# A gated feed-forward block on one core: VectorE's first differences of x in halves, and in another order among its multiplications

## The chip, the core and the metric

The kernel runs on one core of a Trainium2 chip. The metric is the device time of one execution in microseconds (us), from launch to end. Engines are named as in the profile: PE is TensorE, which multiplies matrices; PEld is its loading of weights; DVE is VectorE; ACT is ScalarE; POOL is GpSimd; SP is SyncE, which here only issues DMAs. "L244" is line 244 of the kernel file.

## What is computed

The reference, cut to what matters, with x of 2048 x 1024 (tokens x model width), w_gate and w_up of 1024 x 3584, w_down of 3584 x 1024, all bf16:

```
return (gelu(x @ w_gate) * (x @ w_up)) @ w_down
```

So for each token there are 3584 features; each needs a gate value and an up value, a Gelu of the gate and one multiplication. The last matrix product brings the features back to width 1024.

## The kernel before

**Tiling.** The tokens are taken in two halves of 1024 (`h` = 0, 1), each half as two token blocks of 512 (`tb` = 0, 1). x is held transposed in two tiles, `xT[0]` and `xT[1]`, one per token block: 128 partitions x 8 slices (`kd`) x 512 tokens. Features are taken in blocks of 128, two blocks ("a pair") at a time, so there are 14 pairs per half; weights come in chunks of four blocks, that is two pairs. After the 14 pairs of a half, `down_group` multiplies by w_down for each token block.

**Fewer products.** With the 8 slices of the model width split in two, the two feature blocks and the two token blocks, each pair is a 2 x 2 by 2 x 2 block product, for gate (`j` = 0) and for up (`j` = 1). `pair_quads` computes it in seven products of blocks instead of eight (m1 to m7, four matmuls of 128x128 by 128x512 per product and `j`). The price is sums of blocks. On the side of x there are five, made once per half by `t_sum`, each 128 x 2048 elements in 32-bit form in `t_mem`. With b(j, l) the slices of width half j and token block l: T1 = b(0,1) - b(0,0); T2 = b(1,1) - T1; T3 = b(1,1) - b(0,1); T4 = b(1,0) - T2; and b22, a copy of b(1,1) in 32-bit form. VectorE makes T1 to T4 (L244), ScalarE the copy (L236). On the side of the weights there are S1 to S4 per pair and `j`, of 128 x 512 elements (`s_sum`), made by GpSimd (L365) as a rule, by VectorE (L363) for the first S3, and a copy a22 by ScalarE (L378). The products use them so: m5 is S1 with T1, m6 is S2 with T2, m7 is S3 with T3, m3 is S4 with b22, m4 is a22 with T4, and m1 and m2 use weights and x as they are.

**The first pair.** In half 0, pair 0 is computed without these sums by `first_pair_units` (L311 to L333), since the sums need the whole of x and x is still arriving. It has four units: two feature blocks (`u`) for token block 0, then the same two for token block 1. Each unit holds two of the eight PSUM banks, one for gate and one for up. `part` issues the matmuls (L249): 32 for token block 0, with banks 2, 3 and 6, 7, and 32 for token block 1, with banks 4, 5 for unit 0 and 0, 1 for unit 1. `unit_out` finishes a unit: ScalarE's Gelu of the gate bank (L268), then VectorE's multiplication of that by the up bank into the tile hT (L273). Between them stand the calls of `t_sum`, and behind them the first calls of `s_sum`.

**The pair behind it.** Pair 1 starts with m1, whose result goes to bank 2 (gate) and bank 3 (up) and is then copied by ScalarE (L447) to bank 4 and bank 5. Then m2 is added to banks 2 and 3, so it has to wait for these copies; the copies in turn overwrite banks 4 and 5, which unit 0 of token block 1 still holds until its Gelu (bank 4) and its multiplication (bank 5) have read them:

```
for j in range(2):
    mm(P_[j], j, block(key, j, 0, 0), b11, True)                       # m1
    act(nc.scalar.copy(out=banks[QB[j]][:], in_=banks[P_[j]][:]))      # L447
...
        m2()
```

Then follow m5 (banks 0 and 1, which unit 1 of token block 1 held; copied to a tile by ScalarE, L438), m6 (banks 4 and 5; copied to banks 6 and 7 by ScalarE, L443), then on VectorE the additions of the m5 tile to banks 4 and 5 (L416), then m7, m3 (into banks 4 and 5 behind these additions) and m4. m2's own multiplication into hT and then T4 stand on VectorE's queue ahead of the additions.

**What sets the order.** Each engine runs its instructions in the order in which the calls are made: the helpers `pe`, `dve`, `act`, `pool` and `sp` chain every instruction behind the one before it on the same engine (`on`, L111). An instruction that waits holds up everything behind it on its engine. Waits between engines follow from the tiles that are read and written.

**Loads of x.** The first four slices of xT[0] are transposed by PE and copied out by VectorE (L301) and ScalarE (L303, the last one). The others come by transposing DMAs on SP's queue (L172): four single slices of xT[0], then xT[1] in three: slices 0 and 1, slices 2 and 3, slices 4 to 7.

Of the kernel before, what the change touches and what calls it, by code (L numbers as in the profile page):

```python
# [34 lines left out]
def kernel(  # L35
# [14 lines left out]
    KD = D // P  # L50
    KH = KD // 2
# [71 lines left out]
    def act(inst):  # L123
        return on("act", inst)

    def dve(inst):
        return on("dve", inst)
# [98 lines left out]
    def t_sum(name, c0=0, c1=KH):  # L226
        def b(j, l):
            return xT[l][:, j * KH + c0 : j * KH + c1, :]

        t0 = ("t1", "t2", "t3", "b22", "t4").index(name) * KH * TB  # L230
        t = t_mem[:, t0 : t0 + KH * TB].rearrange("p (a b) -> p a b", b=TB)
        tsum[name] = t
        t = t[:, c0:c1, :]
        if name == "b22":
            for c in range(c1 - c0):
                act(nc.scalar.copy(out=t[:, c, :], in_=b(1, 1)[:, c, :]))  # L236
            return
        in0, in1 = {
            "t1": lambda: (b(0, 1), b(0, 0)),
            "t2": lambda: (b(1, 1), tsum["t1"].bitcast(F32)[:, c0:c1, :]),  # L240
            "t3": lambda: (b(1, 1), b(0, 1)),
            "t4": lambda: (b(1, 0), tsum["t2"].bitcast(F32)[:, c0:c1, :]),
        }[name]()
        dve(nc.vector.tensor_tensor(out=t, in0=in0, in1=in1, op=ALU.subtract))  # L244


    def mm_gu(ps, w_sb, fi, tb, kd):
        pe(
            nc.tensor.matmul(  # L249
                ps[:],  # L250
                lhsT=w_sb[:, kd, fi * P : (fi + 1) * P],
                rhs=xT[tb][:, kd, :],
                start=(kd == 0),
                stop=(kd == KD - 1),
            )
        )
# [3 lines left out]
    def gelu(ps, last=False):  # L260

        if last:
            g_sb = o_pool.tile([P, TB], F32, name="o_sb")[:]
        else:
            e0 = 4 * CH + (g_ctr[0] % 4) * 2 * TB
            g_ctr[0] += 1
            g_sb = w_mem[:, e0 : e0 + 2 * TB].bitcast(F32)
        act(nc.scalar.activation(out=g_sb, in_=ps[:], func=ACT.Gelu_apprx_tanh))  # L268
        return g_sb

    def mult(hT, g_sb, ps, fc, tb):
        dve(
            nc.vector.tensor_tensor(  # L273
                out=hT[:, fc, tb * TB : (tb + 1) * TB],
                in0=g_sb,
                in1=ps[:],
                op=ALU.mult,
            )
        )

    def unit_out(hT, bset, fi, tb):
        mult(hT, gelu(banks[bset[0]]), banks[bset[1]], fi, tb)

    def transpose_x0(q):

        parts = [(2 * q, 0, 4), (2 * q + 1, 0, 4)]
        if q == 0:
            parts = [(0, 0, 2), (0, 2, 4), (1, 0, 4)]
        for n, (kd, ts0, ts1) in enumerate(parts):
            tp = banks[(PB + QB)[(2 * q + n) % 4]][:].bitcast(BF16)  # L290
            for ts in range(ts0, ts1):
                pe(
                    nc.tensor.transpose(
                        tp[:, ts * P : (ts + 1) * P],
                        xs0[:, ts, kd * P : (kd + 1) * P],
                        ident[:],
                    )
                )
            cols = slice(ts0 * P, ts1 * P)
            if q == 0 or n == 0:  # L300
                dve(nc.vector.tensor_copy(out=xT[0][:, kd, cols], in_=tp[:, cols]))  # L301
            else:
                act(nc.scalar.copy(out=xT[0][:, kd, cols], in_=tp[:, cols]))  # L303

    def part(held, tb, k0, k1, us=(0, 1)):
        for kd in range(k0, k1):
            for j in range(2):
                for u in us:
                    mm_gu(banks[held[u][j]], chunks[first][j], u, tb, kd)

    def first_pair_units(hT):  # L311

        held = (VB, RB)
        transpose_x0(0)
        part(held, 0, 0, 1)
        transpose_x0(1)
        part(held, 0, 1, KD)
        for u in range(2):
            unit_out(hT, held[u], u, 0)
        held = (QB, PB)  # L320
        part(held, 1, 0, KH)
        t_sum("t1")
        t_sum("t2")
        t_sum("b22")
        t_sum("t3")
        for u in range(2):
            part(held, 1, KH, KD, (u,))
            unit_out(hT, held[u], u, 1)
        for j in range(2):
            s_sum(0, 1, j, "s3", True, False)  # L330
        for name in ("s1", "s2", "s4"):
            for j in range(2):
                s_sum(0, 1, j, name)  # L333
# [10 lines left out]
    def s_sum(h, pair, j, name, on_dve=False, staged=True):  # L344
        key = (h, "p", pair)

        def a(i, kh):
            return block(key, j, i, kh)

        if on_dve and staged and name in ("s1", "s2", "s3"):  # L350

            if j == 0:
                first_s[name] = wd_pool.tile([P, WDT, D], BF16, name="wd_sb")
            t = first_s[name][:, j, :].bitcast(F32R)
        else:
            s0 = (2 * S_NAMES.index(name) + j) * KH * P
            t = s_mem[:, s0 : s0 + KH * P]
        t = t.rearrange("p (a b) -> p a b", b=P)
        ssum[(h, pair, j, name)] = t

        def tt(in0, in1, op):
            if on_dve:
                dve(nc.vector.tensor_tensor(out=t, in0=in0, in1=in1, op=op))  # L363
            else:
                pool(nc.gpsimd.tensor_tensor(out=t, in0=in0, in1=in1, op=op))  # L365

        if name == "s1":
            tt(a(1, 0), a(1, 1), ALU.add)
        elif name == "s2":
            s1 = ssum[(h, pair, j, "s1")].bitcast(F32)  # L370
            tt(s1, a(0, 0), ALU.subtract)
        elif name == "s3":
            tt(a(0, 0), a(1, 0), ALU.subtract)
        elif name == "s4":
            s2 = ssum[(h, pair, j, "s2")].bitcast(F32)
            tt(a(0, 1), s2, ALU.subtract)
        else:
            act(nc.scalar.copy(out=t, in_=a(1, 1)))  # L378
# [437 lines left out]
    for h in range(NH):  # L816
        hT = hT_pool.tile([P, KF, SH], BF16, name="hT")
        first_pair = 0
        if h == 0:
            first_pair_units(hT)  # L820
            first_pair = 1
            xs = [(tb, kd) for tb in (1, 0) for kd in range(KD)]
            new_x(1)
            stage_load(0)
            stage_load(1)
# [153 lines left out]
```

## Time and profile before

| what | value |
|---|---|
| median of 4 runs | 544.24 us (541.9 to 545.96) |
| the profiled execution: its own time | 545.96 us |
| the profiled execution: span, first to last instruction | 544.2 us |
| granted clock of TensorE | 1.000 |
| PE busy | 532.8 us, 98% of the span |
| DVE, ACT, POOL busy | 362.7, 263.1, 246.6 us |
| T sums on VectorE (L244), 128x2048 each | 2.28 to 3.24 us |
| multiplications of the first units (L273), 128x512 each | 0.67 to 0.69 us |

The profiled execution took 545.96 us, 1.76 us more than its span and 1.72 us more than the median. Of 544.2 us, PE is busy 532.8, so all idle time of PE is some 11 us, and the start and the end of the program hold a good part of that. The stretch that the change touches lies between 12 and 37 us of the span.

### The profile page before, as it was taken

The numbers are of one execution on the slowest core, as the hardware profiler recorded it, in microseconds if no ns is written. First come the engines' busy times: TensorE is split into PE (matmuls) and PEld (weight loads), VectorE is DVE, ScalarE is ACT, GpSimd is POOL, SyncE is SP. The second block draws the span as 40 slices with busy tenths as digits, with TensorE's granted clock in tenths as the row PEclk, the third lists the DMA queues.
The fourth block names the chain that finished last, engine by engine and source line by source line (L and its number), as shares of the span: only waits on it lengthen the run. The fifth ranks groups of instructions, "written<-read, shape, count | busy, mean of one in ns | idle before, by whom it ended". The sixth has DMA issues, their size and how long they took to land.

```text
span 544.2 us, 7084 instructions
## 1 busy us (share of the span) xinstructions
PE 532.8 (98%) x2348; PEld 377.0 (69%) x2384; DVE 362.7 (67%) x472; ACT 263.1 (48%) x446; POOL 246.6 (45%) x212
## 2 busy tenths in 40 slices
PE   8899999998999999999999999999999999999997
PEld 3477777776666677767677666777777766866865
DVE  0986777777676899689584343344444469969951
ACT  1555555554555317216565555555555552452270
POOL 0698777777677000000046777666677740000000
PEclk9999999999999999999999999999999999999999
DMA  9918686696736976879970405041322457677945
GB/s 217 320 33 261 151 275 208 200 275 179 254 125 214 296 236 217 312 226 298 327 233 1 155 1 156 0 155 28 127 87 69 148 187 227 229 243 244 287 148 203
DMA packets 84804, 102.70 MB, mean 189 GB/s; under 512 B 18720, under 2 KB 66336, under 8 KB 84768
## 3 DMA queue, kind: packets, MB, share of 16 engines
q1 hardware_dynamic: 61968, 80.30, 46.7%
q10 hardware_dynamic: 22800, 21.96, 13.1%
q8 instruction: 19, 0.31, 0.2%
q14 instruction: 17, 0.14, 0.1%
HBM read 85.98 MB, written 12.58 MB: 181 GB/s over the span
## 4 chain that ended last, share of the span: by engine, by line
PE 89%; DMA 4%; DVE 4%; issue 2%; ACT 0%; ACTq 0%; SPq 0%; DVEq 0%
PE bank L393 56%; PE bank L667 32%; DMA o_sb<-in_x_dram 2%; DVE t_mem L244 1%; DMA w_mem<-in_w_gate_dram 1%; DVE o_sb L602 1%; DMA w_mem<-in_w_up_dram 1%; DVE s_mem L363 1%; PE bank L249 0%; DVE hT L273 0%; DMA t_dram<-o_sb 0%; DMA x_dram<-o_sb 0%; DVE s_mem L642 0%; DVE bank L416 0%; ACT o_sb L720 0%
## 5 line engine op out<-in xcount | busy, mean ns | idle before, releaser
L393 PE MATMUL bank<-t_mem,s_mem 128*128 128x512 f32 x1056 | 250.0, 394 | 1.8 <-DVE bank L416 1.8
L393 PEld LDWEIGHTS bank<-t_mem,s_mem 128*128 128x128 f32 x1056 | 198.0, 188 | 46.3 <-issue 2.5
L365 POOL TENSOR_TENSOR s_mem<-w_mem 128x512 fp32r<-128x512 bf16 x102 | 121.1, 1209 | 193.8 <-DMA w_mem<-in_w_up_dram 103.3
L273 DVE TENSOR_TENSOR hT<-w_mem,bank 128x512 bf16<-128x512 f32 x104 | 71.0, 686 | 88.5 <-PE bank L393 47.0
L667 PE MATMUL bank<-t_mem,s_mem 128*128 128x512 f32 x544 | 127.2, 392 | 0.0
L667 PEld LDWEIGHTS bank<-t_mem,s_mem 128*128 128x128 f32 x544 | 102.1, 188 | 22.2 <-issue 0.2
L416 DVE TENSOR_TENSOR bank<-bank,m 128x512 f32<-128x512 f32 x108 | 69.6, 694 | 45.4 <-ACT m L438 44.3
L393 PE MATMUL bank<-xT,w_mem 128*128 128x512 bf16 x405 | 96.5, 380 | 3.2 <-ACT bank L447 1.8
L268 ACT ACTIVATE w_mem<-bank 128x512 f32<-128x512 f32 x104 | 61.7, 596 | 57.1 <-DVE bank L416 37.8
L393 PEld LDWEIGHTS <-w_mem 128*128 128x128 bf16 x432 | 40.2, 98 | 53.4 <-issue 8.7
L365 POOL TENSOR_TENSOR s_mem<-w_mem,s_mem 128x512 fp32r<-128x512 bf16 x52 | 65.8, 1290 | 0.0
L577 DVE TENSOR_TENSOR t_mem<-w_mem 128x1024 fp32r<-128x1024 bf16 x56 | 65.6, 1218 | 0.0
L365 POOL TENSOR_TENSOR s_mem<-s_mem,w_mem 128x512 fp32r<-128x512 f32 x52 | 62.3, 1219 | 0.0
L443 ACT COPY bank<-bank 128x512 f32<-128x512 f32 x54 | 30.8, 570 | 38.8 <-PE bank L393 38.5
L378 ACT CAST s_mem<-w_mem 128x512 fp32r<-128x512 bf16 x54 | 33.1, 616 | 31.0 <-PE bank L393 28.8
L642 DVE TENSOR_TENSOR s_mem<-hT 128x512 fp32r<-128x512 bf16 x52 | 35.1, 705 | 10.3 <-PE bank L667 9.5
L438 ACT COPY m<-bank 128x512 f32<-128x512 f32 x54 | 31.7, 587 | 18.0 <-PE bank L393 18.0
L667 PEld LDWEIGHTS <-hT 128*128 128x128 bf16 x224 | 21.3, 98 | 26.6 <-issue 2.1
L447 ACT COPY bank<-bank 128x512 f32<-128x512 f32 x54 | 30.8, 570 | 14.3 <-PE bank L393 12.2
L720 ACT CAST o_sb<-bank 128x512 bf16<-128x512 f32 x28 | 15.4, 585 | 39.9 <-PE bank L667 39.9
L602 DVE TENSOR_TENSOR o_sb<-wd_sb,o_sb 128x512 fp32r<-128x512 bf16 x28 | 29.1, 1038 | 0.5
L574 ACT CAST t_mem<-w_mem 128x1024 fp32r<-128x1024 bf16 x28 | 26.9, 1047 | 0.0
(42 smaller groups left out, 236.9 us busy)
## 6 DMA issues: line engine op xcount, KB each, us to landing
t_mem<-t_dram SPq DMA_DIRECT2D x56, 512.0 KB, 5.4
w_mem<-in_w_gate_dram ACTq DMA_DIRECT2D x10, 1024.0 KB, 5.5
w_mem<-in_w_up_dram ACTq DMA_DIRECT2D x10, 1024.0 KB, 8.6
wd_sb<-in_w_down_dram SPq DMA_DIRECT2D x28, 256.0 KB, 4.8
t_dram<-o_sb SPq DMA_DIRECT2D x28, 256.0 KB, 2.7
wd_sb<-in_w_down_dram SPq DMA_DIRECT2D x12, 512.0 KB, 8.1
w_mem<-in_w_down_dram SPq DMA_DIRECT2D x10, 512.0 KB, 6.2
w_mem<-in_w_down_dram SPq DMA_DIRECT2D x4, 1024.0 KB, 6.6
```

The source lines that it names most:

```text
L268: act(nc.scalar.activation(out=g_sb, in_=ps[:], func=ACT.Gelu_apprx_tanh))
L273: nc.vector.tensor_tensor(out=hT[:, fc, tb * TB : (tb + 1) * TB], in0=g_sb, in1=ps[:], op=ALU.mult,)
L365: pool(nc.gpsimd.tensor_tensor(out=t, in0=in0, in1=in1, op=op))
L378: act(nc.scalar.copy(out=t, in_=a(1, 1)))
L393: nc.tensor.matmul(banks[bank][:], lhsT=lhs[:, c, :], rhs=rhs[:, c, :], start=start and c == 0, stop=c == KH - 1, skip_group_check=True,)
L416: nc.vector.tensor_tensor(out=banks[dst][:], in0=banks[src][:], in1=m5[j][:], op=ALU.add)
L438: act(nc.scalar.copy(out=m5[j][:], in_=banks[V_[j]][:]))
L443: act(nc.scalar.copy(out=banks[RB[j]][:], in_=banks[QB[j]][:]))
L577: dve(nc.vector.tensor_tensor(out=t, in0=in0, in1=in1, op=ALU.subtract))
L602: dve(nc.vector.tensor_tensor(out=t, in0=in0, in1=in1, op=ALU.subtract))
L642: dve(nc.vector.tensor_tensor(out=t, in0=in0, in1=in1, op=op))
L667: nc.tensor.matmul(banks[bset[u]][:], lhsT=lhs(i, u), rhs=rhs(i), start=start and i == 0, stop=stop and i == NS - 1, skip_group_check=True,)
```

## The change

VectorE's queue in `first_pair_units` gets another order, and two of its sums are cut in halves by slices. T1 is made as two instructions of 128x1024 elements (slices 0 and 1, then 2 and 3) and placed ahead of the two multiplications of token block 0's units instead of behind them. T2 stays whole. T3 is also made in two halves: the first is ahead of unit 0's multiplication of token block 1, as the whole was, and the second is between unit 0's and unit 1's. VectorE's queue before: multiplication, multiplication, T1, T2, T3, multiplication, multiplication. After: T1 first half, T1 second half, multiplication, multiplication, T2, T3 first half, multiplication, T3 second half, multiplication. The queues of PE, ACT, POOL and SP hold the same instructions in the same order.

```diff
@@ -315,17 +315,20 @@
         part(held, 0, 0, 1)
         transpose_x0(1)
         part(held, 0, 1, KD)
+        t_sum("t1", 0, KH // 2)
+        t_sum("t1", KH // 2, KH)
         for u in range(2):
             unit_out(hT, held[u], u, 0)
         held = (QB, PB)
         part(held, 1, 0, KH)
-        t_sum("t1")
         t_sum("t2")
         t_sum("b22")
-        t_sum("t3")
-        for u in range(2):
-            part(held, 1, KH, KD, (u,))
-            unit_out(hT, held[u], u, 1)
+        t_sum("t3", 0, KH // 2)
+        part(held, 1, KH, KD, (0,))
+        unit_out(hT, held[0], 0, 1)
+        t_sum("t3", KH // 2, KH)
+        part(held, 1, KH, KD, (1,))
+        unit_out(hT, held[1], 1, 1)
         for j in range(2):
             s_sum(0, 1, j, "s3", True, False)
         for name in ("s1", "s2", "s4"):
```

## The prediction, as it was put on record

> **What bounds the kernel now.** I read the page's busy shares first: PE is busy 532.8 of 544.2 us, at a granted clock of 1.000 throughout, so only PE's gaps can be won. PE's list of waits has six entries, of which two lie where the change is: 1.8 us "<-ACT bank L447" and 0.3 us "<-DVE bank L416" (the latter line also has one of 1.4 us, at 132.9 us). Then PE in order of time (start, duration, what, idle before it and what ended it):
>
> ```profile
> 21.07 2.55 PE L393 MATMUL bank<-xT,w_mem 128*128 128x512 bf16 x11
> 25.46 1.02 PE L393 MATMUL bank<-xT,w_mem 128*128 128x512 bf16 x4 [1.85 <-ACT bank L447]
> 26.14 5.89 PE L393 MATMUL bank<-t_mem,s_mem 128*128 128x512 f32 x24
> 32.36 3.89 PE L393 MATMUL bank<-t_mem,s_mem 128*128 128x512 f32 x16 [0.34 <-DVE bank L416]
> ```
>
> These are m1 and half of m2, the other half of m2, m5 to m7, and m3 with m4 of pair 1. VectorE, and then ScalarE's two L447 rows, over the same stretch:
>
> ```profile
> 14.35 1.29 DVE L273 TENSOR_TENSOR hT<-w_mem,bank 128x512 bf16<-128x512 f32 x2 [7.15 <-PE bank L249]
> 15.55 2.28 DVE L244 TENSOR_TENSOR t_mem<-xT,xT 128x2048 fp32r<-128x2048 bf16 x1
> 17.87 3.13 DVE L244 TENSOR_TENSOR t_mem<-xT,t_mem 128x2048 fp32r<-128x2048 bf16 x1
> 20.92 3.24 DVE L244 TENSOR_TENSOR t_mem<-xT 128x2048 fp32r<-128x2048 bf16 x1
> 24.08 1.27 DVE L273 TENSOR_TENSOR hT<-w_mem,bank 128x512 bf16<-128x512 f32 x2
> 25.27 3.15 DVE L363 TENSOR_TENSOR s_mem<-w_mem 128x512 fp32r<-128x512 bf16 x2
> 28.34 0.68 DVE L273 TENSOR_TENSOR hT<-w_mem,bank 128x512 bf16<-128x512 f32 x1
> 28.94 2.67 DVE L244 TENSOR_TENSOR t_mem<-xT,t_mem 128x2048 fp32r<-128x2048 bf16 x1
> 31.53 2.48 DVE L416 TENSOR_TENSOR bank<-bank,m 128x512 f32<-128x512 f32 x4
> ```
>
> ```profile
> 22.19 0.57 ACT L447 COPY bank<-bank 128x512 f32<-128x512 f32 x1 [0.54 <-PE bank L393]
> 24.84 0.57 ACT L447 COPY bank<-bank 128x512 f32<-128x512 f32 x1 [2.08 <-DVE hT L273]
> ```
>
> VectorE is idle for 7.15 us up to 14.35, then has no gap until 35.4. The multiplication of unit 0, token block 1, starts at 24.08 although its Gelu was done at 19.93, because T2 and T3 stand ahead of it. ScalarE's second copy waits 2.08 us for it, and PE waits for that copy. The chain of waits runs through VectorE's rows from 14.95 to 32.23 and returns to PE at 32.36. So VectorE's queue is the bound from 14 to 32 us, and PE is the bound behind it.
>
> **Why T2, T3 and T4 take 2.7 to 3.2 us where T1 takes 2.28.** GpSimd's rows:
>
> ```profile
> 17.53 1.32 POOL L365 TENSOR_TENSOR s_mem<-w_mem 128x512 fp32r<-128x512 bf16 x1 [16.22 <-DMA w_mem<-in_w_gate_dram]
> 19.31 2.69 POOL L365 TENSOR_TENSOR s_mem<-w_mem 128x512 fp32r<-128x512 bf16 x1 [0.47 <-DMA w_mem<-in_w_up_dram]
> 21.97 4.31 POOL L365 TENSOR_TENSOR s_mem<-s_mem,w_mem 128x512 fp32r<-128x512 f32 x2
> ```
>
> Lay the ends side by side: GpSimd's first sum ends at 18.85, T2 at 21.00, GpSimd's second at 22.00, T3 at 24.16, GpSimd's third at 25.17. The differences are 2.15, 1.00, 2.16, 1.01: the two take strict turns, each blocked while the other works. T4 and both S3 fit the same pattern (S3's own part is 0.55). Multiplications, which read PSUM, keep their 0.6 us step beside GpSimd and take no turn. A sum by turns, then: 2.15 per whole T, 1.1 per half, 0.55 per S3, 1.03 per GpSimd sum.
>
> [...]
>
> **The change, part by part.** *T1 in halves, ahead.* Landing times: slices 0 and 1 of xT[1] were issued at 7.45 and took 4.8 (12.25), slices 2 and 3 at 8.89 and 4.2 (13.09), slices 4 to 7 at 10.24 and 4.7 (14.94). An uncontended 128x1024 sum of bf16 to 32 bits (L577) takes 1.22; half of T1's 2.28, 1.14, is the lower bound. So T1 runs 12.25 to 13.47 and 13.47 to 14.70, in the old idle time. The added waits are for these two landings (and for ScalarE's copy of slice 3 of xT[0], done at 8.73); queued behind them are the multiplications of token block 0, which slip from 14.35 to 14.65 and end at 15.9. Who waits for them: banks 3 and 7, wanted again by m1 at about 21.9 and by ScalarE's L443 copies at 29. That slip costs nothing, with 6 us of cover. T2 starts at 15.85 instead of 17.87, behind its landing of 14.94 and ahead of GpSimd's first sum (17.53), and ends at 18.13 uncontended. The cost of cutting T1 is 2 x 1.22 - 2.28 = 0.16 us of VectorE, in idle time.
>
> *T3 in halves.* GpSimd's first sum has its turn 18.13 to 19.15; T3's first half 19.15 to 20.25; GpSimd's second sum (weights landed at 19.3) 20.25 to 21.3. Unit 0's multiplication runs at 20.2, ends at 20.85, instead of 24.75. T3's second half waits for the turn until 21.3 and ends at 22.4; unit 1's multiplication (Gelu done at 21.65) ends at 23.0 instead of 25.35. The cost of this cut lies between 0 (halves of 1.08) and 0.16 plus one turn of 1.03; I take 0.05 plus the 0.5 that the turns give.
>
> *Behind it.* GpSimd's third sum 22.4 to 23.4, S3 to 23.95, GpSimd's fourth to 25.0, S3 to 25.55, GpSimd's fifth to 26.6, m2's multiplication beside it 25.5 to 26.15, T4 26.6 to 28.75, the addition into bank 4 to 29.35 (31.53 plus 0.62 was 32.15 before).
>
> *What PE sees.* ScalarE's second copy now waits only for m1 itself: in pair 2 the two copies start 0.80 apart (37.23, 38.03), so 22.19 + 0.80 + 0.57 = 23.56, and PE goes on at 23.61 instead of 25.46: **1.85 us** won. m5 follows at 24.3, its second half at 25.2 (bank 1 free at 23.0); m6 at 26.05 and 27.0 (GpSimd's S2 at 23.4 and 25.0); m7 at 27.9 (S3 at 25.55, T3 at 22.4). The last matmul of m7 started at 31.64; at their 0.22 step m3 could have started at 31.86 and did at 32.36. Now it could at 30.01, and the addition is done 0.66 earlier, so the second gap goes as well: **0.5 us** (0.34 listed, the rest hidden in the matmul's modelled end). m3's second half wants GpSimd's sixth sum, which slips from 29.46 to 29.8, at 30.9: covered by 1.1. Sum: 2.35.
>
> *Whether it lasts.* From 32.36 the chain is PE but for one stretch, 110 to 132.9 us. Pair 2's needs move with it: S1 of pair 2 is ready at 30.9 and 32.05, wanted at 35.3; its weights landed at 23.8 and 26.75, wanted at 33.75. The stretch from 110 to 132.9 (a transposing DMA of 9.01 us, a wait of 1.41 at PE) begins with a release by PE's matmuls at 109.9, so it shifts with them.
>
> **The sum.** On the profiled execution's own time: 545.96 - 2.35 = 543.6. It was the slowest of four runs, 1.72 above their median; the gaps won are early and set by fixed work, so I take the same gain off the median: 544.24 - 2.35 = **541.9 us**, or 0.43% less.
>
> **The rivals.**
> *A, half of it (542.6).* VectorE's queue slips where I gave it 0.66 us ahead of need, by a turn lost to GpSimd before T4 (1.03): the addition is then done at 30.4, m3 starts at 30.5. With two turns lost it is 31.5 and the gain 0.9. For it: T3's halves offer one more meeting. Against: every meeting in the trace alternates. Gain 0.9 to 1.9, middle 1.6.
> *B, hidden anyway (544.2).* Something not tied to PE sets a later point, so the gain is given back: the 9.01 us transposes at 116 us are the candidate. For: DMA stands in the chain there. Against: their issue stands behind PE's and VectorE's work in that chain.
> [...]
> *D, more.* The 1.41 us wait at 132.9 goes by luck of the DMAs: 540.5.
> That the queue does not take the written order is excluded: the order of VectorE's instructions in the changed kernel is as the change says, and the other queues are unchanged.
>
> **How the numbers follow.** Chances: forecast 0.60, A 0.18, B 0.12, C 0.05, D 0.05. The range reaches from just below D (540.3) to B (544.2), which takes in A with both its ends and leaves C out. A measurement of this kernel can tell about 0.5% (2.7 us) from no change; the forecast lies at 2.35, just inside, and the four runs spread over 4.06 us, so a median may stand about 1 us off. Faster by over 0.5% (below 541.5): 0.28 from the forecast, 0.03 from A, 0.05 from D, 0.36 in all. Slower by over 0.5% (above 547.0): 0.03, C with that scatter. Within: 0.61.
>
> **What would show it.** Right: L244's first row at 12.2 to 12.5, 128x1024; PE's wait of 1.85 on L447 gone and no L447 wait on L273; the wait at 32.36 gone, m3 at 30.0; the pairs behind it 2.3 us earlier up to 110. Wrong: T1's first half starting after 14 (a landing later than computed), T3's halves with more than one GpSimd sum between them, an addition (L416) that ends after 29.9, or a pair 2 that waits for S sums.

## The result and the profile after

The changed kernel takes 541.94 us (median of 40 runs), the kernel before 544.06 (66 runs). The ratio of the two is 0.997, with a 95% interval of 0.9958 to 0.9983. Of 544.06 us that is 1.6 us, between 0.9 and 2.3. The difference of the medians is 2.1. The runs of each kernel fall in two groups (before: 21 of 66 up to 542.75 us, the others from 543.18 on; changed: 21 of 40 up to 541.96, the others from 542.49 on), so the median of before lies in its upper group and that of the changed kernel in its lower one; the medians of the lower groups are 542.44 and 541.13, 1.3 us apart. On record stood 541.9 and a gain of 2.35.

The profiled execution of the changed kernel has a span of 541.8 us against 544.2. PE, pair 1 and the start of pair 2 (start, duration, what; a bracket would hold idle time before the row):

```profile
19.77 3.63 PE L396 MATMUL bank<-xT,w_mem 128*128 128x512 bf16 x15
23.05 9.52 PE L396 MATMUL bank<-t_mem,s_mem 128*128 128x512 f32 x40
32.41 1.90 PE L396 MATMUL bank<-xT,w_mem 128*128 128x512 bf16 x7
```

m1 and m2 are one row, m5 to m4 another, and neither row has idle time ahead of it. Both gaps of before (1.85 us at 25.46 and 0.34 at 32.36) are gone. VectorE over the same stretch, and below it ScalarE's two copies from m1's banks:

```profile
11.67 2.45 DVE L244 TENSOR_TENSOR t_mem<-xT,xT 128x1024 fp32r<-128x1024 bf16 x2 [4.45 <-DMA xT<-in_x_dram]
14.04 1.28 DVE L273 TENSOR_TENSOR hT<-w_mem,bank 128x512 bf16<-128x512 f32 x2
15.23 2.28 DVE L244 TENSOR_TENSOR t_mem<-xT,t_mem 128x2048 fp32r<-128x2048 bf16 x1
17.43 1.22 DVE L244 TENSOR_TENSOR t_mem<-xT 128x1024 fp32r<-128x1024 bf16 x1
18.66 0.69 DVE L273 TENSOR_TENSOR hT<-w_mem,bank 128x512 bf16<-128x512 f32 x1
19.26 1.49 DVE L244 TENSOR_TENSOR t_mem<-xT 128x1024 fp32r<-128x1024 bf16 x1
20.67 0.68 DVE L273 TENSOR_TENSOR hT<-w_mem,bank 128x512 bf16<-128x512 f32 x1
...
26.98 2.67 DVE L419 TENSOR_TENSOR bank<-bank,m 128x512 f32<-128x512 f32 x4
```

```profile
20.89 0.57 ACT L450 COPY bank<-bank 128x512 f32<-128x512 f32 x1 [0.54 <-PE bank L396]
21.70 0.57 ACT L450 COPY bank<-bank 128x512 f32<-128x512 f32 x1 [0.24 <-PE bank L396]
```

T1's halves lie in what was VectorE's idle time in the profile of before, up to 14.35. (Where token block 0 ends earlier, as in before_again below, VectorE is idle only up to 13.01, and they lie there in part.) Unit 0's multiplication is done at 19.35, so the second copy waits for PE alone, 0.81 behind the first. The additions begin 4.55 us earlier (26.98 against 31.53); 1.30 of that is an earlier start, which is told of next.

One thing in this profile is not the change's. Token block 0's first Gelu starts at 12.41, in the profile of before at 13.71. There PE had a wait of 0.9 us for up weights of the first chunk:

```profile
PE bank L249 <- DMA w_mem<-in_w_up_dram: 0.9, 1, 0.9
```

That transfer took 4.3 us from issue to landing; here it took 3.4, and PE's list has no such wait. So 36.10 - 32.41 = 3.69 us at pair 2 is made of 1.30 us of start and 2.39 us of change. From 132.88 against 129.54 on it is 3.34 (the transpose in the middle took 9.34 us instead of 9.01), and from 492 on 2.3 (a wait of PE of 0.8 us for a load of sums, which the profile of before has not).

To take the start out, I use one measure for all kernels below: **the stretch from token block 0's first Gelu (ScalarE, L268) to the first matmul of pair 2**. It is 22.39 us in the profile of before and 20.00 in that of the changed kernel, where PE has no gap in it.

### The profile page after: what moved, and what is told of

Same layout as the page of the kernel before. It is cut to its first block, busy times and chain, and to the rows that moved or that the text cites. A ratio compares the mean times of both kernels' runs of the same rounds, so it can differ in the third digit from the quotient of the medians.

```text
span 541.8 us, 7086 instructions
## 1 busy us (share of the span) xinstructions
PE 532.6 (98%) x2348; PEld 377.2 (70%) x2384; DVE 361.8 (67%) x474; ACT 263.3 (49%) x446; POOL 245.5 (45%) x212
## 4 chain that ended last, share of the span: by engine, by line
PE 91%; DMA 5%; DVE 2%; issue 1%; ACT 0%; SPq 0%; DVEq 0%; ACTq 0%
PE bank L396 58%; PE bank L670 31%; PE bank L249 2%; DMA o_sb<-in_x_dram 2%; DMA t_mem<-t_dram 1%; DVE o_sb L605 1%; DMA w_mem<-in_x_dram 1%; DMA t_dram<-o_sb 0%; DMA x_dram<-o_sb 0%; DVE hT L273 0%; DVE s_mem L645 0%; DVE s_mem L366 0%; ACT w_mem L268 0%; PE bank L293 0%; DVE t_mem L244 0%
## 5 line engine op out<-in xcount | busy, mean ns | idle before, releaser
L268 ACT ACTIVATE w_mem<-bank 128x512 f32<-128x512 f32 x104 | 61.8, 596 | 54.7 <-DVE bank L419 36.4
L368 POOL TENSOR_TENSOR s_mem<-s_mem,w_mem 128x512 fp32r<-128x512 f32 x52 | 61.2, 1197 | 0.0
L605 DVE TENSOR_TENSOR o_sb<-wd_sb,o_sb 128x512 fp32r<-128x512 bf16 x28 | 30.4, 1084 | 0.5
```

## The experiments

Two theories stood against each other. *Turns:* VectorE's queue ends late because its sums and GpSimd's take turns, and GpSimd's first sums start when their weights land (17.53 and 19.31 us in the profile of before), not when PE is ready; so the gain depends on when the start lets token block 0 end. *Constant gain:* the two gaps are worth 2.35 us always, and what is missing of it was lost later. Beside these stood the question which half of the change does it.

### T1 alone (t1_only)

```diff
-        t_sum("t3", 0, KH // 2)
-        part(held, 1, KH, KD, (0,))
-        unit_out(hT, held[0], 0, 1)
-        t_sum("t3", KH // 2, KH)
-        part(held, 1, KH, KD, (1,))
-        unit_out(hT, held[1], 1, 1)
+        t_sum("t3")
+        for u in range(2):
+            part(held, 1, KH, KD, (u,))
+            unit_out(hT, held[u], u, 1)
```

(against the changed kernel)

> Only T1 in halves ahead of token block 0's multiplications; T3 whole, where it was before. Theory (turns): VectorE's queue is what ends late, and T1 in the idle time takes 2.3 us out of it; where T3 is cut does not matter, since unit 0's multiplication is early enough either way (done at about 20.3 against 21.7 when ScalarE could copy). So the same as the whole change: 1.4 to 2.35 us faster than before, no wait of PE on the L447-copies or on the additions. Rival (each half of the change gives its share): about half the gain, 0.7 to 1.2 us, with a rest of PE's wait on the copy.

541.57 us against 542.68 for the kernel before on the same chip; ratio 0.9984 (0.9961 to 1.0007). PE has no wait in the stretch. In its profile the granted clock was 0.949 and the stretch 20.43 us long; pair 1's first 15 matmuls took 3.76 us there and 3.63 in the changed kernel, the 40 behind them 9.52 in both. I do not lay its length beside the others; the missing waits tell enough. The time alone can tell this neither from the whole change nor from no change.

### T3 alone (t3_only)

The changed kernel with T1 whole and back behind token block 0's multiplications.

> Only T3 in halves around unit 0's multiplication; T1 whole and behind token block 0's multiplications, as before. Theory (turns): unit 0's multiplication comes about 1 to 1.5 us earlier, so PE's first wait (on the L447-copy) goes wholly or mostly; but VectorE's queue ends where it did or a little later (one more instruction, one more turn), so the second wait, on the L416-additions, grows by as much: 0 us, between 0.3 faster and 0.3 slower. Rival (the copy's wait is the loss): 0.9 to 1.85 us faster.

543.51 against 542.68; ratio 1.0008 (0.9991 to 1.0025): no gain. PE:

```profile
20.32 3.63 PE L395 MATMUL bank<-xT,w_mem 128*128 128x512 bf16 x15
23.60 5.87 PE L395 MATMUL bank<-t_mem,s_mem 128*128 128x512 f32 x24
30.69 3.88 PE L395 MATMUL bank<-t_mem,s_mem 128*128 128x512 f32 x16 [1.22 <-DVE bank L418]
```

The wait on the copy is gone, and a wait of 1.22 us on the additions stands in its place. The stretch is 21.44 us. The first wait was what the profile named longest, but it was not what the queue cost: VectorE still did the same work from the same start, and PE met it 24 matmuls later, behind m5, m6 and m7.

### A late start made to order (before_late, after_late, t1_only_late)

```diff
         transpose_x0(1)
+        for _ in range(6):
+            pe(
+                nc.tensor.matmul(
+                    banks[0][:], lhsT=warm_l, rhs=warm_r, start=True, stop=True
+                )
+            )
         part(held, 0, 1, KD)
```

> The kernel before with six idle matmuls of 128x512 (1.3 us) on PE ahead of the last 28 matmuls of token block 0, results unused: token block 0 always ends about 1.3 us later than where the weights come early, and GpSimd's first sums stay where the weights' landing puts them. Theory (the gain depends on the start): 2.0 to 2.4 us slower than before in executions that had no wait for weights, so 1.3 to 2.3 over all; PE's waits on copy and addition as in the profile of before (1.85 and 0.34). Rival (constant gain): 1.3 us slower or less, and no more than its twin with the change loses.

> The changed kernel with the same six idle matmuls. Theory (the gain depends on the start): 1.3 us slower than the changed kernel at most, so 0.2 to 1 us faster than before, and 2.35 us faster than its twin without the change; no wait of PE on copy or addition. Rival (constant gain): the twin differs by what the kernels without idle matmuls differ by, 1.5 us.

> T1 alone in halves ahead, T3 whole, with the six idle matmuls on PE that put token block 0's end 1.3 us later. Theory (turns): T3's halves give nothing at a late start either; unit 0's multiplication is done at about 21.9 to 22.3 against 23.0 to 23.4 when ScalarE can copy, so the stretch from the first Gelu to pair 2 is 20.0 us, as with the whole change and the idle matmuls (19.99), and not 22.5 as without the change. Rival (T3's halves matter where the start is late): 20.4 to 21.5, with a rest of PE's wait on the L447-copy or the L416-additions.

| kernel | time | before, same chip | ratio (95%) | stretch |
|---|---|---|---|---|
| before_late | 545.76 | 542.68 | 1.005 (1.0029 to 1.007) | 22.53 |
| after_late | 542.10 | 542.68 | 1.0002 (0.9979 to 1.0026) | 19.99 |
| t1_only_late | 542.05 | 542.20 | 1.0000 (0.9984 to 1.0017) | 20.00 |

PE of before_late, with both gaps of the first profile again, then PE of t1_only_late:

```profile
25.82 1.02 PE L399 MATMUL bank<-xT,w_mem 128*128 128x512 bf16 x4 [1.77 <-ACT bank L453]
26.50 5.85 PE L399 MATMUL bank<-t_mem,s_mem 128*128 128x512 f32 x24
32.72 3.46 PE L399 MATMUL bank<-t_mem,s_mem 128*128 128x512 f32 x14 [0.37 <-DVE bank L422]
```

```profile
21.01 3.62 PE L400 MATMUL bank<-xT,w_mem 128*128 128x512 bf16 x16
24.29 9.53 PE L400 MATMUL bank<-t_mem,s_mem 128*128 128x512 f32 x40
```

In before_late, T2 (VectorE) and GpSimd's first sum:

```profile
18.09 3.27 DVE L244 TENSOR_TENSOR t_mem<-xT,t_mem 128x2048 fp32r<-128x2048 bf16 x1
18.05 1.15 POOL L371 TENSOR_TENSOR s_mem<-w_mem 128x512 fp32r<-128x512 bf16 x1 [16.75 <-DMA w_mem<-in_w_gate_dram]
```

GpSimd was ahead by 0.04 us, so T2 waited for its sum. By the ratios, 1.3 us of idle matmuls cost the kernel before 2.7 us (1.6 to 3.8; 1.3 to 2.3 were expected), while the changed kernel goes from 0.997 to 1.0002, some 1.7 us, on another chip and with an interval of 1.3 us to either side. The stretches of before_late and its twin after_late differ by 2.54 us and their ratios by 0.0048, which is 2.6 (their medians by 3.66, more than the stretch explains). Each of these ratios is uncertain by 1.1 to 1.3 us, so the times alone leave room for the 1.5 of the rival; the stretches decide. At a late start T1 alone does all that the whole change does, and this with a profile at a granted clock of 1.000: T3's halves add nothing that shows.

### The kernel before, twice more (before_again, before_again2)

> The kernel before, unchanged, for another profile of it. Measured from the first Gelu of token block 0 (ScalarE, L268) to the first matmul of pair 2, the profile of before takes 22.39 us and that of the changed kernel 20.00, in which PE has no gap. Theory (the gain depends on the start): where token block 0 ends early (first Gelu at 12.4), this stretch is 21.4, since GpSimd's turns stay where the weights' landing puts them, so 1.4 is left to win; where it ends at 13.7 or later, 22.3 to 22.5. Rival (constant gain): 22.4 either way.

> The same kernel once more, for a third profile of it, with the same two expectations: 21.4 us with an early end of token block 0 and 22.4 with a late one, against 22.4 either way.

One execution of each, of 546.28 and 542.35 us. First Gelus at 12.38 and 12.73, pair 2 at 33.92 and 34.28: stretches of 21.54 and 21.55, as the first theory has it, so what sets the two executions 3.9 us apart lies outside the stretch. PE in the first of them, and below it T2 and T3 with GpSimd's first two sums:

```profile
19.74 2.55 PE L393 MATMUL bank<-xT,w_mem 128*128 128x512 bf16 x11
23.29 1.02 PE L393 MATMUL bank<-xT,w_mem 128*128 128x512 bf16 x4 [1.01 <-ACT bank L447]
23.97 5.88 PE L393 MATMUL bank<-t_mem,s_mem 128*128 128x512 f32 x24
30.18 3.89 PE L393 MATMUL bank<-t_mem,s_mem 128*128 128x512 f32 x16 [0.33 <-DVE bank L416]
```

```profile
16.54 2.29 DVE L244 TENSOR_TENSOR t_mem<-xT,t_mem 128x2048 fp32r<-128x2048 bf16 x1
18.75 3.24 DVE L244 TENSOR_TENSOR t_mem<-xT 128x2048 fp32r<-128x2048 bf16 x1
18.00 5.00 POOL L365 TENSOR_TENSOR s_mem<-w_mem 128x512 fp32r<-128x512 bf16 x2 [16.69 <-DMA w_mem<-in_w_gate_dram]
```

The first gap is 1.01 us, not 1.85: VectorE's queue started 1.34 us earlier, T2 was under way when GpSimd's first weights landed, and of T2 and T3 only T3 had to wait for a turn. T2 takes 2.29 us instead of 3.13, and these 0.84 us are the difference of the stretches (21.54 against 22.39); in before_late they are 3.27 and 22.53. So of 2.39 us to win, 1.54 are left. Of the eleven profiles of kernels without idle matmuls, the one that the prediction rests on is the only one in which PE itself sits idle for these weights (in before_again, before_again2, the changed kernel and after_again its loading of weights waits for them, for 0.2 to 0.5 us); in the others the first Gelu starts between 12.38 and 12.97.

### The changed kernel once more (after_again)

> The changed kernel unchanged, for another profile and times beside the two others on this chip. Theory (the gain depends on the start): the stretch from the first Gelu to pair 2 is 20.0 us where slices 2 and 3 of xT[1] land by 13.1, and up to 20.9 where they land at 13.7 or later (20.84 in another kernel with the same start); 1.5 us faster than before, between 0.7 and 2.4. Rival (constant gain): 20.0 in any case and 2.35 us faster.

540.89 against 542.12; ratio 0.9965 (0.9944 to 0.9986). The stretch is 20.33. It is not constant: T1's second half waits for slices 2 and 3 of xT[1], and where they land late the whole of VectorE's queue is late. Two kernels below (x_pair, x_first) have the same start as the changed kernel, and t1_whole, the next one, has T1 ahead in one piece. In order of how long after the first Gelu T1 is done:

| kernel | T1 done behind the first Gelu | stretch |
|---|---|---|
| x_pair | 1.67 us | 20.07 |
| changed kernel | 1.71 | 20.00 |
| after_again | 1.90 | 20.33 |
| t1_whole | 2.39 | 20.81 |
| x_first | 2.43 | 20.84 |

In these five, up to about 1.7 us next to nothing is lost; from there on T1's lateness becomes PE's, 0.3 us at 1.90 and 0.8 at 2.4.

### T1 in one piece, ahead (t1_whole)

```diff
-        t_sum("t1", 0, KH // 2)
-        t_sum("t1", KH // 2, KH)
+        t_sum("t1")
         for u in range(2):
             unit_out(hT, held[u], u, 0)
```

> The change with T1 in one piece ahead of the multiplications: it has to wait for slices 2 and 3 (landing at about 13.1) and so starts some 0.9 to 1.2 us later than the first half did. Theory (turns): token block 0's multiplications and T2 end 0.7 to 1.1 us later, GpSimd's first sum then comes ahead of more of VectorE's work, and of the gain 0.2 to 1.3 us is left where the start is early. Rival (the order alone matters): the same as the whole change.

542.12 against 542.33; ratio 0.9987 (0.9969 to 1.0005), which the time alone tells neither from the whole change nor from no change. In this execution slices 2 and 3 landed early (12.7), and T1 still ended 2.39 us behind the Gelu, with 0.54 us of PE's second wait left. From the rows, the halves of T1 are worth what the second landing is later than the first, less the 0.16 us of the cut, and at most 1.06 us (2.29 less one half of 1.23), an estimate. Their rows in x_first, where that landing came 4.8 us behind its issue, at 13.7:

```profile
11.81 1.23 DVE L244 TENSOR_TENSOR t_mem<-xT,xT 128x1024 fp32r<-128x1024 bf16 x1 [4.71 <-DMA xT<-in_x_dram]
13.68 1.23 DVE L244 TENSOR_TENSOR t_mem<-xT,xT 128x1024 fp32r<-128x1024 bf16 x1 [0.65 <-ACT w_mem L268]
```

(The releaser named in the second row is not what was waited for: the instruction reads nothing of that Gelu's, and its start falls together with the landing.)

### GpSimd's turns taken away (no_turns)

```diff
         key = (h, "p", pair)
+        if (h, pair) == (0, 1) and name in ("s1", "s2", "s4"):
+            ssum[(h, pair, j, name)] = tsum["t1"][:, :, 0:P]
+            return
```

(against the kernel before; S1, S2 and S4 of pair 1 are left out, and the result is another)

"Port" in the expectation stands for whatever VectorE and GpSimd take turns at; the runs show the turns, and none shows what that is.

> The kernel before without GpSimd's six sums for pair 1: S1, S2 and S4 of that pair are left out, and its matmuls read columns of T1 in their place (same shapes, another result). VectorE's order is that of before. Theory (turns of the port): T2 and T3 then take 2.28 us each instead of up to 3.24, unit 0's multiplication is done when ScalarE can copy, and the stretch from token block 0's first Gelu to pair 2's first matmul is 20.0 to 20.4 us as in the changed kernel, against 21.5 to 22.5 in three profiles of before; 1.2 to 2.2 us faster than before. Rival (T2 and T3 are slow by themselves, or from the transfers of that time): 3.1 and 3.2 us again and a stretch of 21.5 or more.

540.47 against 542.12; ratio 0.9974 (0.9953 to 0.9996); stretch 20.01, and no wait of PE in it. VectorE:

```profile
16.58 2.29 DVE L244 TENSOR_TENSOR t_mem<-xT,t_mem 128x2048 fp32r<-128x2048 bf16 x1
18.79 2.28 DVE L244 TENSOR_TENSOR t_mem<-xT 128x2048 fp32r<-128x2048 bf16 x1
...
22.19 1.29 DVE L366 TENSOR_TENSOR s_mem<-w_mem 128x512 fp32r<-128x512 bf16 x2
```

T3 takes 2.28 us instead of 3.24, two S3 take 1.29 instead of 3.13 (before_again), in the old order and with the same transfers issued. The cause of the late queue is GpSimd's six sums, and at this start (first Gelu at 12.43) the order of before would have been good enough without them.

### Two tries at PE's wait in the middle (x_first, x_pair)

The largest wait that PE has left is 1.4 us at 129.5 us. x_first issues the transposes of the next x ahead of weights and stores; x_pair gives two of them one buffer:

```diff
-                    then.get("m2 of last", [])
-                    + steps[:2]
-                    + [lambda q=q: stage_x(*q) for q in xs[:2]]
+                    [lambda q=q: stage_x(*q) for q in xs[:2]]
+                    + then.get("m2 of last", [])
+                    + steps[:2]
```

```diff
...
-        t = o_pool.tile([P, 1, TB], BF16, name="o_sb")
+        if kd % 2 == 0:
+            x_pair[:] = [o_pool.tile([P, 2, TB], BF16, name="o_sb")]
+        t = x_pair[0][:, kd % 2 : kd % 2 + 1, :]
...
```

> The changed kernel with another order in pairs 2 to 9 of half 0: the transposing DMAs of the next x are issued ahead of the weight chunk and of the stores of sums, not behind them. It aims at PE's wait of 1.4 us at 129.5, behind a transpose of 9.3 us that is issued with a chunk of weights in flight. If that transfer is slow because of the chunk, the wait goes and it is 1.0 to 1.4 us faster than the changed kernel, 2.5 to 3 us faster than before. If the tile's reuse is what binds, no change, or slower by the other order of the four buffers.

> The changed kernel with one buffer instead of two for the two transposed slices of the next x that each of pairs 6 to 9 stages (both fit in one). It aims at PE's wait of 1.4 us at 129.5, which goes back to a buffer that is still held by a slow transpose. If the number of buffers binds: that wait is gone, 1.0 to 1.4 us faster than the changed kernel in most executions, some 2.7 us faster than before. If not: the same as the changed kernel.

x_first: 542.28 against 542.33, ratio 0.9996 (0.998 to 1.0012), so no gain over before shows, where 2.5 to 3 us would have meant that the order was it. The wait of 1.40 us moved to 104.9, where the chain now goes through a load of weights of 9.85 us. x_pair: 540.80 against 542.12, ratio 0.9972 (0.9955 to 0.9989), the same as after_again on that chip (540.89). In its profile the wait was there as before:

```profile
129.57 3.91 PE L396 MATMUL bank<-t_mem,s_mem 128*128 128x512 f32 x16 [1.40 <-DVE bank L419]
```

So neither the other order nor the other number of buffers was a gain; what brings the wait about stays open, and one profile of each kernel cannot say more. In the fourteen profiles it shows no tie to the change: it was 1.4 us in the profiles of before, the changed kernel, t3_only, t1_whole and x_pair, 2.3 in before_again, before_late and after_late, and missing in before_again2, after_again, no_turns, t1_only and t1_only_late. No version tried is clearly faster than the changed kernel.

## Why the prediction was right, and where it was not

*What bounds the kernel* held: VectorE's queue from 14 to 32 us, through turns with GpSimd (no_turns shows it: without them T3 takes 2.28 us instead of 3.24). The turns are those of the profile of before (ends 2.15, 1.00, 2.16 and 1.01 us apart), and they held in the changed kernel. There GpSimd's first sum is

```profile
17.71 1.96 POOL L368 TENSOR_TENSOR s_mem<-w_mem 128x512 fp32r<-128x512 bf16 x1 [16.40 <-DMA w_mem<-in_w_gate_dram]
```

It ends at 19.67, a second behind T3's first half (18.65). T3's second half, which starts at 19.26 in VectorE's rows, waited for it and took 1.49, some 0.4 more than half of a T alone, where 0.5 was put down. GpSimd's second sum ends at 21.76, a second behind that half (20.75). The first half had its turn ahead of GpSimd's first sum, not behind it as written; at a late start (after_late) it was as written, and that half took 2.18 us.

*T1 in halves* held: landings of 4.1 and 4.0 us (4.8 and 4.2 put down), halves of 1.22 to 1.23 (1.22), and the slip of token block 0's multiplications cost nothing. That T1 lies in idle time held, nearly, at a late start alone. There T2 starts 1.98 us behind the first Gelu (after_late) instead of 4.15 (before_late), 2.2 earlier; at the usual start it is 2.82 (changed kernel) instead of 4.16 (before_again), 1.3 earlier: T1 waits for the landings of x, however early PE ends.

*T3 in halves* was written as a step that brings unit 0's multiplication from 24.75 to 20.85. By itself that is worth nothing: with T1 ahead and T3 whole, unit 0's multiplication is early enough (t1_only_late, 20.00 us), and without T1 ahead the halves only move the wait (t3_only, 21.44). The sum did not ask what each half was worth.

*What PE sees* held for the execution it was made from: 2.35 forecast, 2.39 between the profiles once the start is taken out, 2.54 between the twins with a late start.

*The step that failed* is this sentence of the sum: "the gaps won are early and set by fixed work, so I take the same gain off the median". They are not set by fixed work. One side of the race is tied to the landing of weights (GpSimd's first sum starts between 17.3 and 18.7 us in the profiles, at 17.53 in the one in hand), the other starts when PE ends token block 0, and the profile in hand was the one of eleven with a late end. The wait of 0.9 us that made it late is one of the six entries that the prediction counted in PE's list, and it took no account of it. At the usual start 21.55 us are to be cut to 20.0 to 20.84, a gain of 0.7 to 1.55, not 2.35. The measured 1.6 (0.9 to 2.3) agrees with that, and 2.35 lies just outside. That 541.9 met 541.94 owes something to chance: the four runs shown had a median of 544.24, the 66 runs one of 544.06, and the difference of medians (2.1) is larger than the ratio (1.6) and the lower groups (1.3) say. Beside the kernel before on other chips the changed kernel's median is 1.2 us lower (after_again), that of T1 alone 1.1.

*The rivals.* A named a smaller gain (0.9 to 1.9), and its size is about right, but its cause, a turn lost before T4, did not occur: the turns alternate wherever I followed them row by row. (The middle of its ends is 1.4, not 1.6 as written.) B did not occur; the lead at pair 2 is kept to 110 us. C, the slower kernel with its chance of 0.05, did not occur. D, the missing wait in the middle, does occur in some executions, with the change and without.

## What to carry to other kernels

Before a gain is taken from a gap in one profile, ask what each side of the gap is tied to: if one is tied to a transfer's landing and the other to an engine's progress, the gap is the difference of two times that move apart from each other, and it can have another size in the next execution, so look at a second profile of the same kernel (here 2.39 us were to be won in one profile and some 1.5 in each of the next two). Removing the wait that the profile names longest is worth nothing while the queue behind it still ends at the same time (t3_only: no wait on the copy, 1.22 us on the additions in its place, a ratio of 1.0008); work moved into that engine's idle time is what counts (t1_only_late: a stretch of 20.00 us against 22.53 in before_late). In these runs sums on VectorE and GpSimd side by side cost each other whole turns (a T of 2.28 us took up to 3.27, a GpSimd sum of 1.16 up to 3.2), so the first place for VectorE's SBUF work is where GpSimd is still waiting for its data (T2 took 2.29 us in before_again, where it started ahead of that landing, and 3.13 in the profile of before, where it started behind it).

## What the runs showed of the hardware

In the rows followed, VectorE's SBUF-to-SBUF sums and GpSimd's alternate strictly while both have work: a T of 128x2048 takes 2.28 to 2.29 us alone (no_turns) and up to 3.27 with one GpSimd sum ahead of it (T2 in before_late), and a GpSimd sum of 128x512 takes 1.16 alone (35.95 in the profile of before) and up to 3.2 behind a whole T (21.97 there, behind T3). VectorE's multiplications with a PSUM operand stay at 0.6 us a step in either case: two take from 24.08 to 25.27 in the profile of before, with GpSimd at work, and from 20.99 to 22.19 in no_turns, without.

Six idle matmuls (1.3 us) put on PE cost the kernel before 2.7 us (1.6 to 3.8), about twice their own time; in its profile the stretch was 0.99 us longer (22.53 against 21.54), which is what T2 took longer (3.27 against 2.29) behind one GpSimd sum.

VectorE's sums with bf16 operands and a 32-bit result took 1.22 to 1.23 us for 128x1024 (T1's halves in the changed kernel, x_pair, x_first and t1_only_late) and 2.28 to 2.29 for 128x2048 (T1 and T3 in no_turns), so a cut in two costs 0.16 us (2 x 1.22 - 2.28).
